# Output projection of the first attention block on 64-row tiles, in two-step turns with sixteen row maxima; 32 turns with six

## The chip, the core and the metric

The kernel runs on one core of a Trainium2 chip. TensorE (PE) multiplies into PSUM, VectorE (DVE) and ScalarE (ACT) read PSUM, GpSimd (POOL) works on SBUF only, SyncE (SP) issues the DMAs. PSUM has eight banks of 128 x 512 float32. The metric is the device time in microseconds (us), as the median of several runs. The profile is one execution of the same program.

## What is computed

Two attention blocks on inputs of 2048 tokens and width 512, with 32 heads of 16 channels. Block A sees a window of 256 tokens, block B sees all 2048. The results stand side by side.

```python
qkv = (x @ wqkv).reshape(B, S, 3, H, Dh).transpose(2, 0, 3, 1, 4)
scores = einsum("bhqd,bhkd->bhqk", q, k) * Dh ** -0.5    # A: where(mask, scores, -1e9)
o = einsum("bhqk,bhkd->bhqd", softmax(scores), v)
out = o.transpose(0, 2, 1, 3).reshape(B, S, D) @ wo
```

Float32 accuracy comes from splitting operands into a high and a low part: each product of the projections is three matmuls (high x high, high x low, low x high).

## The kernel before

The program has two stages. The first, up to about 518 us, does block A and the projections of both blocks, in an order written out by hand (`ORDER_A`). The second stage, of which the change speaks, is one Python loop that writes out block B's attention: 32 units (8 head groups of 4 heads, 4 chunks of 512 queries), each of 16 key steps of 128 keys, so 512 steps. One turn of the loop covers two steps and follows the string `ORDER`, one letter for each piece of work:

- `s`: one score product, 128 keys x 512 queries of one head (`scores`, a matmul with 51 rows on one 64-row tile of PE), then ScalarE's exponential of the 128x512 block into `p` (L635). Eight in a turn.
- `m`: the row maxima of one head over 512 keys: a matmul with 48 rows on one 64-row tile (`max2`, L471) and VectorE's reduction of 128x512 (L475). `M`: the same for two heads, with one reduction of 128x1024. Four `m` and two `M` are eight maxima in a turn. They belong to the next unit: the scores of a unit need its maxima, which go through GpSimd (`max_chunk`, `max_finish`), a transpose on PE (`max_rows`, L595) and a DMA into `oq`.
- a digit: that many 128-query quarters of a step of the weighted sum of the values (`weigh2`, L659), on four 32-column tiles of PE. Eight quarters in a turn.

Two matmuls on the two 64-row tiles run side by side, so two of `s` and `m` take one slot of PE.

Meanwhile block A's result is projected with `wo`: 16 output tiles of 128 x 512 (`project_out`), each 4 x 3 matmuls with 128 rows (`products`, L222), a copy by ScalarE (L779) and a DMA. When two tiles are due, the loop writes both out after the digit `4` of a turn, 24 matmuls in a row with nothing between. This happens in eight turns. No row maxima are issued during these 24 matmuls.

PSUM in this loop: bank 0 is the weighted sum, banks 1 to 3 go to scores in turn, 4 and 5 to `M`, 6 and 7 to `m` and to the output tiles in turn. A matmul waits until its bank has been read. Each engine works in its own order; nothing is reordered at run time, so a waiting matmul holds up all of PE's queue behind it.

After the last maxima the loop follows the string `LAST`, with block B's first output tiles in it.

Of the kernel before, what the change touches and what calls it, by code (L numbers as in the profile page):

```python
# [41 lines left out]
ORDER = "ssm4mssMs2msms2sM"  # L42
LAST = "4ssssfssss4"
AHEADM = 4
# [37 lines left out]
class Model:  # L82
# [64 lines left out]
    def release(self, bank, t):  # L147
        self.banks[bank[0]][bank[1]] = t + self.load


@with_exitstack
def attention_kernel(ctx: ExitStack, tc: tile.TileContext, xT, wqk, wv, wo, out):
# [190 lines left out]
    def half_rows(stage, pairs, banks):  # L343

        turn, q0 = divmod(CHUNK * stage, 12)
        for q in range(q0, q0 + CHUNK):
            k, i = divmod(q, 3)
            u, v = ((0, 0), (0, 1), (1, 0))[i]
            for a in range(2):
                l, r = pairs[a ^ turn][k]  # L350
                rows = slice(64 * a, 64 * a + 64)
                op = nc.tensor.matmul(view(banks[a ^ turn]), l(u)[rows], r(v)[rows], start=turn == q == 0,  # L352
                                      stop=turn == 1 and q == 11)
                if turn and q == a == 0:
                    tc.add_manual_dep(op.ins, min(since)[2].ins.name, LANDED, reason="the row tiles change banks")
        M.pe("h", CHUNK * 233)

# [89 lines left out]
    def maxima(b, g, c):  # L447

        if not b:
            if (b, g, c) not in mt:  # L450
                xt.reverse()
                mt[b, g, c] = xt[0]
            return mt[b, g, c].rearrange("p a s (r q) -> p a r q s", q=4)
        if (b, g, c) not in mt:
            m = sb.tile([128, NQC, HG, 4], F32, name=f"mt_{b}_{g}_{c}",
                        **(dict(tag="mte", bufs=1) if (b, g, c) == (1, 0, 0) else dict(tag="mt", bufs=3)))
            mt[b, g, c] = m.rearrange("p k h q -> p h q k")
        return mt[b, g, c]

    def max2(g, c, qt, kc, heads, ps):  # L460

        m = maxima(1, g, c).rearrange("p (a r) q k -> p a r q k", a=2)
        early = g == 0 and c == 0 and heads[0] < 2
        if not early:
            follow(("k", 1, g))
            follow(("q", 1, g, c))
        for n, j in enumerate(heads):
            r, a = divmod(j, 2)
            rows = slice(ROW[a], ROW[a] + KS)
            q, k = (qe[0], ke()) if early else (opq[1, g, c][:, r], opk2(g)[:, r])  # L470
            nc.tensor.matmul(ps[:, n], q[rows, 128 * qt:128 * qt + 128], k[rows, kc * QC:kc * QC + QC], start=True,  # L471
                             stop=True)
            t = M.pe("h", 118, 0 if early else loaded(1, g, c))
        r, a = divmod(heads[0], 2)
        op = nc.vector.tensor_reduce(out=m[:, a:a + len(heads), r, qt, kc], in_=ps, axis=AX.X, op=ALU.max)  # L475
        return mark(op, M.run("DVE", 65 + 533 * len(heads), t))
# [23 lines left out]
    def max_item(b, g, c, qt, j, kc):  # L500
        n = f"{b}_{g}_{c}_{qt}_{j}_{kc}"
        if b:
            banks, two = take2()
            release2(banks, max2(g, c, qt, kc, (j, j + 1), two))
# [28 lines left out]
    def max_chunk(b, g, c, kc):  # L533

        n = f"{b}_{g}_{c}"
        m = mt[b, g, c]
        if kc == 1:
            parts["mm"] = sb.tile([128, HG, 4], F32, name=f"mm_{n}", tag="mm")
        mm = parts["mm"]
        x = m[:, :, :, kc]  # L540
        up = sb.tile([128, HG, 4], F32, name=f"mu_{n}_{kc}", tag="mu", bufs=1)
        gt = sb.tile([128, HG, 4], F32, name=f"mg_{n}_{kc}", tag="mg", bufs=1)

        if kc == 1:
            nc.gpsimd.tensor_sub(up, x, m[:, :, :, 0])  # L545
        else:
            nc.gpsimd.tensor_add(up, x, mm)
        nc.gpsimd.tensor_scalar(gt, up, 0.0, None, op0=ALU.is_gt)
        nc.gpsimd.tensor_mul(up, up, gt)
        if kc == 1:  # L550
            nc.gpsimd.tensor_add(up, up, m[:, :, :, 0])
# [5 lines left out]
    def max_finish(b, g, c):  # L557
# [7 lines left out]
        if slot[0]:  # L565
            mr = max_chunk(b, g, c, 3)
            r1 = sb.tile([128, HG, 4], F32, name=f"nr_{n}", tag="nr")
            mr, r1 = (y.rearrange("p (a r) q -> p a (r q)", a=2) for y in (mr, r1))
# [4 lines left out]
        else:  # L573
            if b:
                nc.vector.tensor_reduce(out=x[:, :, 0], in_=mt[b, g, c].rearrange("p (a r) q k -> p a (r q) k", a=2),
# [8 lines left out]
    def max_rows(b, g, c):  # L584
        n = f"{b}_{g}_{c}"
        nm = parts["nm"].bitcast(BF16).rearrange("p a s (n u) -> p a (s n) u", u=2)[:, :, :, 1]
        if slot[0]:

            bank = M.take("e")
            ps = view(bank)  # L590
# [27 lines left out]
    def scores(b, g, c, kt, j, heads=1, pieces=((),)):  # L618
# [3 lines left out]
        banks = [M.take("e" if b else "u") for _ in range(heads)]  # L622
        ps = [view(bank) for bank in banks]
# [10 lines left out]
        for x in range(heads):  # L634
            op = nc.scalar.activation(p[:, a0 + x, :w], ps[x][:, :w], AF.Exp, scale=SCALE)  # L635
            done = mark(op, M.run("ACT", 60 + w / 1.2, t))
            M.release(banks[x], done)
# [124 lines left out]
    def project_out(b, c, qts):  # L762
# [14 lines left out]
        for qt in qts:  # L777
            ob = row(f"ob_{b}_{c}_{qt}")
            nc.scalar.activation(ob, ps[qt], AF.Copy)  # L779
            t = M.run("ACT", 480, M.t["PE"] + WAKE)  # L780
            release(banks[qt], t)
            nc.sync.dma_start(out[c * QC + 128 * qt:c * QC + 128 * qt + 128, b * D:(b + 1) * D], ob)
            M.dma(256, t)
# [211 lines left out]
    for u, (b, g, c) in enumerate(units[:NA + 2]):  # L995
        its = max_items(b, g, c)
        its = its[:HG // 2 * AHEADM] if u > NA else [it for it in its if it[1]] if u == NA else its
# [162 lines left out]
    M.banks["e"] = M.banks["u"][:3]  # L1160
    slot[0] = True
    steps = [(g, c, kt) for _, g, c in units[NA:] for kt in range(NT)]
    turn = len(units) - NA - 1
    mx = [(NA + 1 + i // 16, *units[NA + 1 + i // 16][1:], *divmod(i % 16, NQC)) for i in range(16 * turn)]
    ns, nq, nm, half, got = 0, -8, AHEADM, 0, 0
    t0 = M.t["PE"]
    half_tile = 0
    rows = []
    while nq < 4 * len(steps):
        if nm == len(mx) and len(M.banks["e"]) == 3:  # L1170

            M.banks["e"] += [M.t["PE"] + 3000] * 2
        for x in ORDER if nm < len(mx) else LAST:
            k = ns // HG
            if x == "s" and k < len(steps):
                if ns % HG == 0:
                    t = k * STEP
                    M.t["PE"] = max(M.t["PE"], t0 + int(1000 * k * STEP))
# [3 lines left out]
                scores(1, *steps[k], ns % HG)  # L1182
                ns += 1
            elif x in "Mm" and nm < len(mx):
                if nm == AHEADM and got == 0:
                    for _ in range(FILL):
                        nc.tensor.matmul(ps_all[:, 0, 0:256], mone[:, 0], mone, start=True, stop=True)
                u, g, c, qt, kc = mx[nm]
                if x == "M":
                    h = (0, 1)  # L1190
                    two = view(("p", 0))
                else:
                    h = (2 + half,)
                    half ^= 1
                    two = room()[1][:, None]
                max2(g, c, qt, kc, h, two)
                got += len(h)
                if got == HG:
                    nm += 1
                    got = 0  # L1200
                    if nm % 16 in (14, 15):
                        max_chunk(1, g, c, nm % 16 - 13)
                    if nm % 16 == 0:
                        max_finish(1, g, c)
                        rows.append((k + 1, (1, g, c)))
            elif x == "f" and k < len(steps) and not rows:

                for _ in range(6):
                    if gen[0] or proj and proj[0][0] <= k * STEP and operands(proj[0][3]) <= M.t["PE"]:
                        advance()  # L1210
                        half_tile += 1
# [3 lines left out]
            elif x.isdigit():  # L1215
                if 0 <= nq < 4 * len(steps):
                    g, c, kt = steps[nq // 4]
                    q = nq % 4
                    weigh2(g, c, kt, 128 * q, 128 * (q + int(x)))
                    if kt == NT - 1 and q + int(x) == 4:  # L1220
# [46 lines left out]
```

## Time and profile before

| | |
|---|---|
| device time, median of 3 runs | 1799.53 us (1796.18 to 1802.74) |
| span of the profiled execution | 1797.4 us |
| what lies around the span, by the median | 2.1 us |
| PE, DVE, ACT, POOL busy in the span | 99%, 84%, 78%, 36% |
| second stage, from the first to the last turn with maxima | 520.5 to 1716.3 us |
| an ordinary turn (800 to 986.3 us are 40 of them) | 4.66 us |
| the 40 turns that hold the eight with output tiles | 581.2 to 813.2 us |

The busy share of PE is an upper bound, since the ends of matmuls are modelled. The distance between the starts of two rows is read instead. In a view by order of time a row merges equal instructions that follow each other; it gives the start of the first, the time from there to the end of the last, and their count.

### The profile page before, as it was taken

The page shows a single profiled execution, that of the slowest core. Times are in us where ns is not written, and L with a number is a line of the kernel's source. Part 1 is how long each engine was busy: PE and PEld are TensorE (multiplying, and loading weights), DVE is VectorE, ACT ScalarE, POOL GpSimd, SP SyncE. Part 2 cuts the span into 40 slices and gives each one's busy share as a digit, 9 for nine tenths or more (in the row PEclk, how much of TensorE's full clock was granted, in tenths as well). Part 3 has the DMA queues.
Part 4 walks back from the last instruction along what each step waited for, and adds up shares of the span by engine and source line. Part 5 has one row for each costly group of instructions (what it writes and reads, how often), then busy time and mean ns, then how long its engine had stood idle before and what let it go on. Part 6 is the DMA issues. An engine that isn't in the chain of part 4 may idle for free.

```text
span 1797.4 us, 39182 instructions
## 1 busy us (share of the span) xinstructions
PE 1779.1 (99%) x15054; PEld 907.9 (51%) x15054; DVE 1510.2 (84%) x2244; ACT 1401.6 (78%) x2749; POOL 651.4 (36%) x1334
## 2 busy tenths in 40 slices
PE   8999999999999999999999999999999999999999
PEld 6776657767754555444444444444444444444336
DVE  4766786676789677899999999999999999999911
ACT  4366676665569677899999999999999999999983
POOL 0377888656755331133400024220112422022220
PEclk9999999999999999999999999999999999999999
DMA  7766667645562223211200310130031121010012
GB/s 256 204 204 202 202 203 224 177 143 172 187 183 87 78 86 100 52 41 37 65 17 31 72 34 29 38 70 16 17 77 35 29 64 37 17 54 9 32 37 94
DMA packets 129354, 166.80 MB, mean 93 GB/s; under 512 B 23204, under 2 KB 59044, under 8 KB 129156
## 3 DMA queue, kind: packets, MB, share of 16 engines
q1 hardware_dynamic: 129168, 164.31, 31.0%
q8 instruction: 118, 1.93, 0.4%
q14 instruction: 68, 0.56, 0.1%
HBM read 94.49 MB, written 68.19 MB: 91 GB/s over the span
## 4 chain that ended last, share of the span: by engine, by line
PE 94%; DMA 2%; ACT 1%; DVE 1%; SPq 1%; issue 1%; POOL 0%; ACTq 0%; DVEq 0%
PE ps_all L659 30%; PE ps_all L471 20%; PE ps_all L628 19%; PE ps_all L222 11%; PE ps_all L352 7%; PE ps_all L674 4%; PE ps_all L518 3%; ACT p L635 1%; DMA in<-xT_A 1%; SPq L382 0%; PE ps_all L595 0%; DVE nm L528 0%; DMA in<-xT_B 0%; DVE ps_all L527 0%; DMA vd<-vst 0%
## 5 line engine op out<-in xcount | busy, mean ns | idle before, releaser
L635 ACT ACTIVATE p<-ps_all 128x512 f32<-128x512 f32 x2432 | 1260.9, 597 | 178.8 <-PE ps_all L628 114.6
L475 DVE TENSOR_REDUCE mt<-ps_all 128x2 f32<-128x1024 f32 x1516 | 1195.6, 870 | 63.0 <-PE ps_all L471 63.0
L628 PE MATMUL ps_all<-oq,opk 51*128 51x512 f32 (+2 forms) x2752 | 768.4, 404 | 4.5 <-ACT p L635 2.4
L471 PE MATMUL ps_all<-opk,oq 48*128 48x512 f32 x2016 | 673.3, 438 | 0.2
L659 PE MATMUL ps_all<-p,vt 128*17 128x256 f32 (+1 forms) x6056 | 586.2, 460 | 1.7 <-ACT ou L685 1.7
L628 PEld LDWEIGHTS ps_all<-oq,opk 51*128 51x128 f32 x2752 | 394.6, 185 | 179.0 <-ACT p L635 150.3
L471 PEld LDWEIGHTS ps_all<-opk,oq 48*128 48x128 f32 x2016 | 307.7, 184 | 315.3 <-DVE mt L475 179.5
L645 POOL TENSOR_SCALAR_AFFINE_SELECT p<-p 128x256 f32<-128x256 f32 x480 | 179.8, 409 | 110.7 <-ACT p L635 108.8
L659 PEld LDWEIGHTS ps_all<-p,vt 128*17 128x17 f32 x6056 | 101.5, 95 | 228.1 <-issue 215.7
L545 POOL TENSOR_TENSOR mu<-mt 128x16 f32<-128x16 f32 x31 | 6.9, 221 | 509.3 <-DVE mt L475 509.3
L527 DVE COPY_PREDICATED ps_all<-mone,ps_all 128x256 f32<-128x256 uint16 x224 | 95.3, 426 | 82.0 <-PE ps_all L518 75.4
L528 DVE TENSOR_REDUCE nm<-ps_all 128x2 f32<-128x512 f32 x224 | 155.2, 693 | 7.7
L713 POOL TENSOR_TENSOR rd<-ld,minus 128x32 f32<-128x32 f32 x15 | 81.9, 5460 | 216.4 <-DMA ld<-od 216.4
L352 PE MATMUL ps_all<-x,w 64*128 64x512 f32 x720 | 119.1, 392 | 0.0
L222 PE MATMUL ps_all<-x,w 128*128 128x512 f32 x408 | 104.3, 405 | 2.9 <-ACT x L170 2.2
L674 PE MATMUL ps_all<-p,vt 128*17 128x384 f32 (+2 forms) x1408 | 94.1, 387 | 0.1
L518 PE MATMUL ps_all<-opk,oq 48*128 48x384 f32 (+2 forms) x512 | 91.8, 362 | 2.2 <-DMA oq<-parts 0.7
L222 PE MATMUL ps_all<-w_o,x_o 128*128 128x512 f32 x384 | 92.5, 395 | 0.0
L352 PEld LDWEIGHTS ps_all<-x,w 64*128 64x128 f32 x720 | 84.1, 185 | 8.8
L222 PEld LDWEIGHTS ps_all<-x,w 128*128 128x128 f32 x408 | 75.3, 191 | 25.8 <-ACT x L170 2.9
L305 ACT ACTIVATE raw<-ps_all 128x512 f32<-128x512 f32 x56 | 32.3, 597 | 70.4 <-PE ps_all L222 55.5
L222 PEld LDWEIGHTS ps_all<-w_o,x_o 128*128 128x128 f32 x384 | 70.7, 188 | 25.0 <-issue 8.4
(77 smaller groups left out, 942.2 us busy)
## 6 DMA issues: line engine op xcount, KB each, us to landing
parts<-st SPq DMA_DIRECT2D x64, 512.0 KB
oq<-parts SPq DMA_DIRECT2D x128, 128.0 KB
opk<-parts SPq DMA_DIRECT2D x128, 128.0 KB
od<-ou SPq DMA_DIRECT2D x64, 256.0 KB
vd<-vst SPq DMA_DIRECT2D x32, 272.0 KB
oq<-parts SPq DMA_DIRECT2D x128, 64.0 KB
opk<-parts SPq DMA_DIRECT2D x128, 64.0 KB
t<-od SPq DMA_DIRECT2D x32, 256.0 KB
```

What stands on the lines that cost most here:

```text
L222: nc.tensor.matmul(ps, l(u), r(v), start=start and k == 0, stop=stop and k == n - 1)
L352: op = nc.tensor.matmul(view(banks[a ^ turn]), l(u)[rows], r(v)[rows], start=turn == q == 0, stop=turn == 1 and q == 11)
L471: nc.tensor.matmul(ps[:, n], q[rows, 128 * qt:128 * qt + 128], k[rows, kc * QC:kc * QC + QC], start=True, stop=True)
L475: op = nc.vector.tensor_reduce(out=m[:, a:a + len(heads), r, qt, kc], in_=ps, axis=AX.X, op=ALU.max)
L518: nc.tensor.matmul(two[:, a, 0:w], opq[b, g, c][rows, r, 128 * qt:128 * qt + 128], opk2(g)[rows, r, t0:t1], start=True, stop=True)
L527: nc.vector.copy_predicated(two[:, :, 256:384], later, two[:, :, 0:128])
L528: op = nc.vector.tensor_reduce(out=m[:, :, r, qt, 0], in_=two[:, :, 128:384], axis=AX.X, op=ALU.max)
L628: nc.tensor.matmul(ps[x][:, col:col + n1], opk2(g)[rows, pr, 128 * k:128 * k + 128], opq[b, g, c][rows, pr, q0:q0 + n1], start=True, stop= ...
L635: op = nc.scalar.activation(p[:, a0 + x, :w], ps[x][:, :w], AF.Exp, scale=SCALE)
L645: nc.gpsimd.affine_select(out=v, in_=v, pattern=[[0, 2], [sign, 128]], compare_op=ALU.is_ge, fill=zero_fill, base=base, channel_multiplier ...
L659: nc.tensor.matmul(o[32 * j:32 * j + VW, q0:q1], vt[(g // 2) % 2][:, kt, vc:vc + VW], pts[1, g, c, kt, j // 2][:, j % 2, q0:q1], start=kt ...
L674: nc.tensor.matmul(o[32 * j:32 * j + VW, q0:q0 + w], vt[(g // 2) % 2][:, kt, vc:vc + VW], pts[b, g, c, m, j // 2][:, j % 2, col:col + w], ...
```

## The change

The output tiles of block A are written in pairs on 64-row tiles: a 128-row matmul becomes two with 64 rows, one on each tile of PE (`half_step`, which the first stage had inside `half_rows`). In the first 12 of 24 steps the upper row tile works on the first output tile and the lower one on the second, then they change over; the first matmul after that waits for an operation (the earliest by the planner's clock) issued since, so that both tiles never write one bank. The 24 steps (`g`) stand between the letters of a turn of its own, `OUTS`, with 16 maxima, all of single heads, 8 scores and 8 quarters (two digits `4` in a row). Both tiles are copied by ScalarE behind the last `g` (`put_out`).

Maxima that are thus done early let 32 other turns be `FEW`, with 6 maxima and two digits `4`, while `MANY` is the old `ORDER` unchanged. A turn is `FEW` when the maxima lead the scores by more than 1.25 units (`LEADM`). The program as built has, in order, 14 turns `MANY`, then 40 turns that are 8 `OUTS` and 32 `FEW` (OOFFFFOFOFFFFOOFFFFOFOF and 17 more F), then 192 `MANY` and 10 `LAST`; before, all 246 turns up to `LAST` were `ORDER`.

The maxima of a unit now run with the key chunk as the outer loop, so that `max_chunk` runs after each quarter of a unit and no longer at its end. Banks are chosen by a small model of the engines (`Loop`): scores use banks 1 to 4 in `FEW`, maxima 5 to 7; in `OUTS` both share 1 to 5 and the output tiles hold 6 and 7. `PACES` is a planner's clock that says when loads and other side work are written out.

```diff
-ORDER = "ssm4mssMs2msms2sM"
+MANY = "ssm4mssMs2msms2sM"
+FEW = "msmms4msssmsm4ss"
+OUTS = "mgggmmggmsgggmsgmmgmggmm44smgsmmgggsgsmggmssggmggg"
 LAST = "4ssssfssss4"
-AHEADM = 4
+PACES = {FEW: 2.25, MANY: 2.45, OUTS: 5.4, LAST: 2.45}
+ROOMS = {FEW: (range(4), range(4, 7)), MANY: (range(3), range(5, 7)), OUTS: (range(5), range(5)),
+         LAST: (range(5), range(5))}
+LEADM = 1.25
...
+class Loop:
...
+    def pick(self, rooms, ready=0):
+        n = min(rooms, key=lambda n: (self.free[n], n))
+        return n, max(ready, self.free[n] + self.SEM)
...
+    def half_step(q, pairs, ps):
+
+        turn, q = divmod(q, 12)
+        k, i = divmod(q, 3)
+        u, v = ((0, 0), (0, 1), (1, 0))[i]
+        for a in range(2):
+            l, r = pairs[a ^ turn][k]
+            rows = slice(64 * a, 64 * a + 64)
+            op = nc.tensor.matmul(ps[a ^ turn], l(u)[rows], r(v)[rows], start=turn == q == 0,
+                                  stop=turn == 1 and q == 11)
+            if turn and q == a == 0:
+                tc.add_manual_dep(op.ins, min(since)[2].ins.name, LANDED, reason="the row tiles change banks")
...
+    def put_out(b, c, qt, ps):
+        ob = row(f"ob_{b}_{c}_{qt}")
+        nc.scalar.activation(ob, ps, AF.Copy)
+        t = M.run("ACT", 480, M.t["PE"] + WAKE)
+        nc.sync.dma_start(out[c * QC + 128 * qt:c * QC + 128 * qt + 128, b * D:(b + 1) * D], ob)
...
     while nq < 4 * len(steps):
...
+        two = heapq.nsmallest(2, proj)
+        lead = np_ / 32 - ns / 64
+        if np_ == total:
+            cycle = LAST
+        elif two and two[-1][0] <= ns / HG * STEP and max(operands(x[3]) for x in two) <= M.t["PE"]:
+            cycle = OUTS
...
+        else:
+            cycle = FEW if lead >= LEADM + 1 / 32 else MANY
+        loop.rooms = ROOMS[cycle]
+        for x in cycle:
...
+            elif x == "g":
+                if nh == 12:
+                    ready_h = max(ready_h, loop.first + loop.SEM)
+                half_step(nh, [pairs_out(*y) for y in two], [ps_all[:, 6], ps_all[:, 7]])
...
+                if nh == 12:
+                    since.clear()
+                    loop.first = M.NEVER
+                if nh == 24:
+                    for n1, y in enumerate(two):
+                        put_out(*y, ps_all[:, 6 + n1])
...
-                if int(x) == 4 and nm < len(mx):
-
-                    t = k * STEP
-                    two = heapq.nsmallest(2, proj)
-                    if two and two[-1][0] <= t and max(operands(y[3]) for y in two) <= M.t["PE"]:
-                        now[0] = t
-                        for _ in two:
-                            advance()
-                            while gen[0]:
-                                advance()
-                            t0 += 2400
```

In the rows of the program's order below, `w_o` is a part of `wo`, `x_o` a normalised part of block A's result, `oq` and `opk` the operands of scores and maxima, `p` the exponentials and `vt` the values. What stands in brackets are the engines and DMA queues whose semaphores the row waits for.

On PE, at the first pair of output tiles, before:

```order
L659 MATMUL ps_all<-p_0_1_10_0_7788,vt_77 17x512 x2
L659 MATMUL ps_all<-p_0_1_10_1_7801,vt_77 17x512 x2
L222 MATMUL ps_all<-w_o_6439,x_o_0_0_7299 128x512 [waits DVE_49]
L222 MATMUL ps_all<-w_o_6439,x_o_0_0_7299 128x512 x2
L222 MATMUL ps_all<-w_o_6468,x_o_1_0_7403 128x512 [waits Pool_49]
L222 MATMUL ps_all<-w_o_6468,x_o_1_0_7403 128x512
L222 MATMUL ps_all<-w_o_6468,x_o_1_0_7403 128x512 [waits Pool_49]
```

On PE, at the same pair, now:

```order
L557 MATMUL ps_all<-opk_75,oq_0_3_6956 128x512 [waits DMAHW4_49,DMAHW3_49,Activation_49]
L440 MATMUL ps_all<-w_o_6439,x_o_0_0_7313 128x512 [waits DVE_49] x2
L440 MATMUL ps_all<-w_o_6439,x_o_0_0_7313 128x512 x4
L557 MATMUL ps_all<-opk_75,oq_0_3_6956 128x512 [waits DMAHW6_49,DMAHW5_49,Activation_49]
L557 MATMUL ps_all<-opk_75,oq_0_3_6956 128x512 [waits Activation_49]
L440 MATMUL ps_all<-w_o_6468,x_o_1_0_7346 128x512 x4
L557 MATMUL ps_all<-opk_75,oq_0_3_6956 128x512 [waits DVE_49]
L713 MATMUL ps_all<-oq_0_1_6572,opk_75 128x512
```

The output matmuls (L222, now L440 and twice as many) no longer stand in one run: maxima (L557) and scores (L713) stand between them.

On PE, where the second output tile of a pair begins, before:

```order
L222 MATMUL ps_all<-w_o_6777,x_o_3_0_7568 128x512 [waits Pool_49]
L222 MATMUL ps_all<-w_o_6439,x_o_0_0_7299 128x512 [waits DVE_49]
L222 MATMUL ps_all<-w_o_6439,x_o_0_0_7299 128x512 x2
L222 MATMUL ps_all<-w_o_6468,x_o_1_0_7403 128x512 x3
L222 MATMUL ps_all<-w_o_6686,x_o_2_0_7433 128x512 x3
```

On PE, where the row tiles change over in the same pair, now:

```order
L745 MATMUL ps_all<-p_0_1_11_0_7815,vt_77 17x512 x2
L745 MATMUL ps_all<-p_0_1_11_1_7828,vt_77 17x512 x2
L713 MATMUL ps_all<-oq_0_1_6572,opk_75 128x512 [waits DVE_49]
L557 MATMUL ps_all<-opk_75,oq_0_3_6956 128x512 [waits DVE_49]
L440 MATMUL ps_all<-w_o_6439,x_o_0_0_7313 128x512 [waits Activation_49]
L440 MATMUL ps_all<-w_o_6439,x_o_0_0_7313 128x512
L713 MATMUL ps_all<-oq_0_1_6572,opk_75 128x512 [waits DVE_49]
```

The 13th step waits for ScalarE, with a score two places ahead of it. In four of the eight pairs the 13th step names ScalarE, in the other four VectorE.

On PE, behind the last matmul of a pair of output tiles, before:

```order
L222 MATMUL ps_all<-w_o_6777,x_o_3_0_7568 128x512 x3
L471 MATMUL ps_all<-opk_75,oq_0_3_6956 128x512 [waits DMAHW6_49,DMAHW5_49,Activation_49]
L628 MATMUL ps_all<-oq_0_1_6572,opk_75 128x512 x2
L471 MATMUL ps_all<-opk_75,oq_0_3_6956 128x512 x2
L628 MATMUL ps_all<-oq_0_1_6572,opk_75 128x512
L659 MATMUL ps_all<-p_0_1_11_0_7815,vt_77 17x256 x2
```

On PE, behind the second pair, where a turn `FEW` follows, now:

```order
L440 MATMUL ps_all<-w_o_6777,x_o_3_0_7568 128x512 x6
L557 MATMUL ps_all<-opk_75,oq_0_3_6956 128x512 [waits DVE_49]
L713 MATMUL ps_all<-oq_0_2_6760,opk_75 128x512 [waits DMAHW3_49]
L557 MATMUL ps_all<-opk_75,oq_0_3_6956 128x512 [waits Activation_49] x2
L713 MATMUL ps_all<-oq_0_2_6760,opk_75 128x512 [waits DMAHW4_49]
L745 MATMUL ps_all<-p_0_1_14_0_7997,vt_77 17x512 x2
```

Two maxima that wait for ScalarE now stand among the first four matmuls behind the pair.

## Rows read from the trace of the kernel before

**Rows 1.** First part of the page: busy time, share of the span, instructions.

```profile
PE 1779.1 (99%) x15054; PEld 907.9 (51%) x15054; DVE 1510.2 (84%) x2244; ACT 1401.6 (78%) x2749; POOL 651.4 (36%) x1334
```

**Rows 2.** Two stretches of 40 turns: us, busy PE PEld DVE ACT POOL, clock, DMA.

```profile
581.23:813.18 231.95, 231.95 (x1808) 111.13 (x1804) 187.76 (x241) 177.00 (x347) 66.56 (x126) 1.00 0.25 71
800.00:986.30 186.30, 186.30 (x1614) 75.62 (x1610) 186.30 (x242) 168.86 (x331) 45.13 (x106) 1.00 0.15 39
```

**Rows 3.** DVE by order of time, an ordinary turn: start, us, operation, count.

```profile
1004.31 0.68 DVE L475 TENSOR_REDUCE mt<-ps_all 128x1 f32<-128x512 f32 x1
1004.91 0.68 DVE L475 TENSOR_REDUCE mt<-ps_all 128x1 f32<-128x512 f32 x1
1005.51 1.22 DVE L475 TENSOR_REDUCE mt<-ps_all 128x2 f32<-128x1024 f32 x1
1006.64 0.68 DVE L475 TENSOR_REDUCE mt<-ps_all 128x1 f32<-128x512 f32 x1
```

**Rows 4.** PE by order of time, an ordinary turn.

```profile
1009.03 0.50 PE L471 MATMUL ps_all<-opk,oq 48*128 48x512 f32 x1
...
1009.37 0.39 PE L471 MATMUL ps_all<-opk,oq 48*128 48x512 f32 x1
...
1009.61 0.40 PE L471 MATMUL ps_all<-opk,oq 48*128 48x512 f32 x1
1009.93 0.62 PE L659 MATMUL ps_all<-p,vt 128*17 128x256 f32 x8
1010.49 0.50 PE L471 MATMUL ps_all<-opk,oq 48*128 48x512 f32 x1
...
1011.16 0.63 PE L659 MATMUL ps_all<-p,vt 128*17 128x256 f32 x8
1011.72 0.50 PE L628 MATMUL ps_all<-oq,opk 51*128 51x512 f32 x1
...
1012.64 1.05 PE L659 MATMUL ps_all<-p,vt 128*17 128x512 f32 x8
1013.62 0.49 PE L471 MATMUL ps_all<-opk,oq 48*128 48x512 f32 x1
```

**Rows 5.** A turn with a pair of output tiles, PE, ACT and DVE.

```profile
585.93 5.74 PE L222 MATMUL ps_all<-w_o,x_o 128*128 128x512 f32 x24
...
589.03 0.60 ACT L779 ACTIVATE ob<-ps_all 128x512 f32<-128x512 f32 x1 [2.95 <-POOL nm L569]
...
591.60 0.50 PE L471 MATMUL ps_all<-opk,oq 48*128 48x512 f32 x1
...
592.04 0.60 ACT L779 ACTIVATE ob<-ps_all 128x512 f32<-128x512 f32 x1 [2.41 <-PE ps_all L222]
592.13 3.02 DVE L475 TENSOR_REDUCE mt<-ps_all 128x1 f32<-128x512 f32 x4 [5.41 <-PE ps_all L471]
```

**Rows 6.** DVE's waits from 575 to 770 us: total, times, longest.

```profile
DVE mt L475 <- PE ps_all L471: 44.2, 9, 5.7
```

**Rows 7.** ACT by order of time, exponentials without a pause between.

```profile
1009.60 2.56 ACT L635 ACTIVATE p<-ps_all 128x512 f32<-128x512 f32 x5 [0.41 <-PE ps_all L471]
```

**Rows 8.** First stage, PE by order of time: products on 64-row tiles.

```profile
118.91 1.54 PE L352 MATMUL ps_all<-x,w 64*128 64x512 f32 x12
120.29 0.34 PE L518 MATMUL ps_all<-opk,oq 48*128 48x384 f32 x2
```

**Rows 9.** PE by order of time, a turn with the transpose of a unit's maxima.

```profile
1006.33 0.63 PE L659 MATMUL ps_all<-p,vt 128*17 128x256 f32 x8
1006.92 0.23 PE L595 MATMUL ps_all<-ident,nm 128*32 128x128 bf16 x2
1007.08 0.50 PE L628 MATMUL ps_all<-oq,opk 51*128 51x512 f32 x1
```

More of the change, by code (lines that the diff above doesn't have):

```diff
@@ L343, in half_rows @@
     def half_rows(stage, pairs, banks):
[L345 to L355, printed above, removed]
-        M.pe("h", CHUNK * 233)
+        for q in range(CHUNK * stage, CHUNK * stage + CHUNK):
+            half_step(q, pairs, [view(bank) for bank in banks])
+        M.pe("h", CHUNK * 233)
+    def half_step(q, pairs, ps):
+        turn, q = divmod(q, 12)
+        k, i = divmod(q, 3)
+        u, v = ((0, 0), (0, 1), (1, 0))[i]
+        for a in range(2):
+            l, r = pairs[a ^ turn][k]
[4 more added lines that the diff above has]
+                tc.add_manual_dep(op.ins, min(since)[2].ins.name, LANDED, reason="the row tiles change banks")
     def heads_of(b, g, s, a):
@@ L503, in max_item @@
             banks, two = take2()
-            release2(banks, max2(g, c, qt, kc, (j, j + 1), two))
+            release2(banks, max2(g, c, kc, qt, j // 2, (0, 1), two))
             return
@@ L565, in max_finish @@
         if slot[0]:
[L566 to L568 removed]
+            mr = max_chunk(g, c, 3)
+            r1 = sb.tile([128, 16], F32, name=f"nr_{n}", tag="nr")
+            mr, r1 = (y.rearrange("p (a n) -> p a n", a=2) for y in (mr, r1))
             nc.gpsimd.tensor_copy(nm[:, :, :, 1], mr)
@@ L587, in max_rows @@
         if slot[0]:
-            bank = M.take("e")
-            ps = view(bank)
+            bank, ps = None, ps_all[:, 1 + loop.rows()]
         else:
@@ L621, in scores @@
         pr, a0 = divmod(j, 2)
-        banks = [M.take("e" if b else "u") for _ in range(heads)]
-        ps = [view(bank) for bank in banks]
+        if b:
+            ps = [ps_all[:, 1 + loop.score(a0)]]
+        else:
+            banks = [M.take("u") for _ in range(heads)]
+            ps = [view(bank) for bank in banks]
         w = QC if b else sum(x[3] for x in pieces)
@@ L777, in project_out, with pairs_out @@
         for qt in qts:
[L778 to L783, printed above, removed]
+            release(banks[qt], put_out(b, c, qt, ps[qt]))
+    def put_out(b, c, qt, ps):
[3 more added lines that the diff above has]
+        nc.sync.dma_start(out[c * QC + 128 * qt:c * QC + 128 * qt + 128, b * D:(b + 1) * D], ob)
+        M.dma(256, t)
+        return t
+    def pairs_out(b, c, qt):
+        return [(lambda u, p=p: osp[b, p, c][:, u, 128 * qt:128 * qt + 128], lambda v, p=p: ws[b, "o", p][:, v])
+                for p in range(NG // 2)]
     units = [(b, g, c) for b in range(2) for g in range(NG) for c in range(NQC)]
@@ L1159, in attention_kernel @@
     M.load = 0
-    M.banks["e"] = M.banks["u"][:3]
+    loop = Loop()
     slot[0] = True
     steps = [(g, c, kt) for _, g, c in units[NA:] for kt in range(NT)]
-    turn = len(units) - NA - 1
-    mx = [(NA + 1 + i // 16, *units[NA + 1 + i // 16][1:], *divmod(i % 16, NQC)) for i in range(16 * turn)]
-    ns, nq, nm, half, got = 0, -8, AHEADM, 0, 0
+    total = 32 * NA
+    ns, nq, np_, nf = 0, -8, 40, 0
+    side, other = 1, None
     t0 = M.t["PE"]
```

163 lines of the change are left out of this document (116 added, 47 removed).

## The prediction

> **What bounds the kernel now.** I read the page first, and saw that its shares do not decide: PE is busy for 99% of the span and DVE for 84% [rows 1], and the first is an upper bound. So I read the second stage by stretches of 40 turns. In an ordinary stretch, 186.3 us, DVE is busy for all of it; in the stretch that holds the eight pairs of output tiles it is busy for 187.8 of 231.95 us [rows 2]. Three facts follow.
>
> First, an ordinary turn is DVE's. The starts show .60 us for a single reduction (1004.31 to 1004.91) and 1.13 for a double (1005.51 to 1006.64) [rows 3]. Four and two of them are 4 x .60 + 2 x 1.13 = 4.66, and 186.3 / 40 is 4.66 [rows 2].
>
> Second, PE is hardly behind. In order of time its turn is a run of row-tile matmuls of three slots (1009.03 to 1009.93, .90), a weighted sum of two quarters (.56), two slots (.67), .56, three slots (.92) and a sum of four quarters (.98, 1012.64 to 1013.62), together 4.59 [rows 4]. A slot, two matmuls side by side, is .235 us (1009.37 to 1009.61 is .24); a run of n slots takes about .20 more than n x .235, for the changes of mode at its ends [rows 4].
>
> Third, the pairs leave DVE idle. 24 output matmuls run from 585.93 to 591.60 and DVE's next reduction has waited 5.41 us [rows 5]; all such waits are 44.2 us [rows 6], which is 231.95 - 187.76. That is the most that the change could win.
>
> **The change part by part.** I sum over the same 40 turns, 231.95 us before; they hold 320 maxima before and after (8 x 16 + 32 x 6), and DVE needs 320 x .60 = 192 us for them as singles. Outside, the other 206 turns with maxima and `LAST` keep their contents. The order on every engine up to the first pair is the old one but for the maxima's layout; I cost that at nothing, because the reductions of the same shapes hide it.
>
> *A turn FEW.* DVE falls to 6 x .60 = 3.6 us. ACT needs 8 x .49 = 3.9, since five exponentials take 2.56 us of which the last is .60 [rows 7]. PE has two runs of seven matmuls, which need four slots each (.235 x 4 + .20 = 1.14), and two sums of four quarters (.98): 2 x 2.12 = 4.25. So PE sets it, and a turn gains .41. 32 x 4.25 = 136.0. No row shows such a turn; the bounds are 4.23, with no jitter, and 4.45, if scores also wait for ACT now and then (below).
>
> *A turn OUTS, PE alone.* 24 steps are 24 slots; the twelve half-rows that the first stage runs take 1.38 us to the next row (118.91 to 120.29), .23 a slot [rows 8], so 64-row halves cost the .236 of a 128-row matmul (5.67 / 24, [rows 5]) and nothing is won on PE as such. 16 maxima and 8 scores are 12 slots, and about half a slot goes unused where two neighbours want the same row tile: 36.5 x .235 + .20 = 8.78. Eight quarters in a row are .98 + .88 = 1.86 (the .10 of the way out falls once). 10.64 a turn, 8 x 10.64 = 85.1. DVE's 16 x .60 = 9.6 lies beside it.
>
> *The output banks behind a pair.* This is the term that I look at hardest. Before, the first tile's copy starts at 589.03, under the second tile's matmuls; what follows on PE goes to other banks first, so the second copy, at 592.04, holds up nothing for a while [rows 5]. Now both tiles end with the same slot. A matmul's start to its copy's start is .5 us (half the run is over at 588.77, so the 12th of 24 starts at 588.53, its copy at 589.03), the copy is .60 [rows 5], the next start behind a wait takes .10 longer [rows 4], and the second copy comes .49 later [rows 7]. PE can write the first bank 1.2 and the second 1.7 us after the last step. But the order puts maxima for these banks, or the next pair, one to two slots behind it: some .5. So PE stands still for about 1.2, with everything queued behind. 8 x 1.2 = 9.6; the bounds are .5 a turn, if only one bank is wanted early, and 1.3: 4 to 10.4.
>
> *The changeover.* The 13th step waits for an earlier operation. In four pairs it names ScalarE, with a score two places ahead: .5 to the exponential, .60 for it, .10 more, less the slot that is due anyway: 1.0. In the others it names a reduction that should be old. Where ACT's operation is older than that score, less is left, so I take .6 x 4 = 2.5, between 0 and 8.
>
> *The rest.* The first pair finds both banks in VectorE's hands, and maxima at the ends of `OUTS` turns wait for reductions: 1.5 in all, between 0 and 4. Each unit's transpose lengthens PE's turn from .56 to .75 (1006.33 to 1007.08) [rows 9]; DVE covered that and PE's turns do not: 5 units x .19 = 1.0. The loads that `PACES` moves on SP are the same in number; I cost them at nothing, since units of maxima lead by over one, and a late load would cost one stall of 1 to 2 us.
>
> Sum: 136.0 + 85.1 + 9.6 + 2.5 + 1.5 + 1.0 = 235.7 against 231.95: **+3.8 us**. The span becomes 1801.2, and with the 2.1 us by which the median stands above the profiled span, 1803.3. The change thus trades DVE's idle 44.2 us for PE's limit: PE's pure work would gain 10 us, and new waits eat it.
>
> Two rules of the Trainium skill speak against the change. The pair's copies are seen at 589.03 and 592.04, three microseconds apart [rows 5]. The page TensorEngine Tiling (Array Packing), in Performance Considerations under PSUM Bottleneck, says that tiling speeds up TensorE but not the emptying of PSUM, which may become the limit. By it the term of 9.6 stands; without it the sum would be 226.1, a gain of 5.9. No row of before shows a changeover's wait in this loop. The same page, in Restrictions and Gotchas, Gotcha 1, says that different row tiles cannot use one PSUM bank at the same time and that software has to see to it. By it the changeover's wait cannot be left out; if all eight pairs pay it in full the sum is 241.2.
>
> **The rivals.** *A, the waits are covered.* If copies and the changeover fall under work that PE has anyway, 136.0 + 85.1 + 1.0 = 222.1 is left, -9.9: 1789.7. For it: ACT is idle for half of an `OUTS` turn, so copies start at once. Against it: the order itself, since nothing on PE stands between. 12%.
>
> *B, slower, by the score banks in FEW.* PE issues seven matmuls in a row of which four are scores, on four banks; ACT hands a bank back each .49 us [rows 7], and stands only .35 a turn below PE's 4.25. If ACT starts each half turn late, behind .98 of weighted sums, PE waits some .1 each half turn: 4.45, 32 x .2 = 6.4 more, 1809.7. It decides from .04 a turn upwards, with the sum near the bound. Against it: four banks, and three carry an ordinary turn without a wait in its slots [rows 4]. 22%.
>
> *C, slower, by the changeover*: all eight pairs wait 1.0, +5.5: 1808.8. Against it are the four that name VectorE. 12%.
>
> That the change does not do what it says is ruled out by the order: eight pairs, 384 half-row matmuls.
>
> **How the numbers follow.** Forecast 54%, 1803.3, with its own range 1798 to 1808. A measurement can tell .3%, 5.4 us, from no change: 1794.1 to 1804.9. Of the forecast's 54%, some 41 fall within this and 12 above; A gives 11 below; B and C are mostly above, 9 of their 34 within. So faster 12%, same 50%, slower 38%. The range: with 4, 0 and 0 for the waits the sum ends at 226.1, 1793.7; with B's price on top and the waits at 10.4 and 4, about 1812. I take 1793 to 1812.
>
> **What would show it.** In the changed kernel's trace: `FEW` turns of 4.2 to 4.3 us, with PE and no longer DVE without idle time; `OUTS` turns of 11 to 12.6; behind each pair a stop of PE that ends with ACT's copy, about 1.2; at the 13th step, in four pairs, one that ends with an exponential; ordinary turns still 4.66. The forecast is wrong if `FEW` turns are above 4.4 (B), or if `OUTS` turns come to 10.7 with no stop behind (A). The weakest terms are the stop behind a pair and the price of a `FEW` turn: .1 us in each of the latter is 3.2 us.

## The result and the profile after

The changed kernel takes 1804.26 us (median, 1800.56 to 1809.47) against 1799.49 for the kernel before on the same chip (1796.18 to 1803.50): a ratio of 1.0027, 95% interval 1.0018 to 1.0035. That is 4.8 us slower, just inside the .3% that was called no change, and 1.0 us above the forecast. The profiled execution has a span of 1802.6 us (before 1797.4).

First part of the page of the changed kernel:

```profile
PE 1779.8 (99%) x14926; PEld 913.2 (51%) x14926; DVE 1524.2 (85%) x2324; ACT 1403.5 (78%) x2749; POOL 648.6 (36%) x1334
```

Against [rows 1] next to nothing moved: DVE has 80 reductions more and 14 us more of work, PE's busy time is the same within 1 us. The stretch tells more. Two stretches of the changed kernel, from the first maximum of the first turn `OUTS` to the first score of the first `MANY` behind (the same 40 turns as before, with the same 320 maxima), and 186 us behind it (columns as in [rows 2]):

```profile
584.75:820.14 235.39, 230.65 (x1677) 115.25 (x1673) 203.56 (x323) 179.17 (x347) 63.24 (x124) 1.00 0.22 64
820.14:1006.40 186.26, 186.14 (x1607) 75.58 (x1607) 184.17 (x238) 168.59 (x330) 40.86 (x102) 1.00 0.15 38
```

The 40 turns take 235.39 us against 231.95 [rows 2]: +3.44; the sum said 235.7. The rest of the 5.2 us between the spans lies outside: the first pair's turn begins .8 us later, and 1.0 is lost behind 820.14, part of it where the first `MANY` waits for its three score banks. The .8 can't be put down to the change: in the profiles of the experiments below that leave everything ahead of the first pair as it is in the changed kernel, the first output matmul starts between 581.2 and 588.8 us. DVE's idle time in the stretch fell from 44.2 [rows 6] to 235.39 - 203.56 = 31.8 us, and PE, busy without a break before, now has 4.7 us without a matmul even by its modelled ends.

Where that is, is read from starts. PE by order of time behind the second pair, and ACT at the same place:

```profile
608.67 0.86 PE L440 MATMUL ps_all<-w_o,x_o 64*128 64x512 f32 x6
609.65 0.49 PE L557 MATMUL ps_all<-opk,oq 48*128 48x512 f32 x1
609.65 0.49 PE L713 MATMUL ps_all<-oq,opk 51*128 51x512 f32 x1
610.28 0.98 PE L557 MATMUL ps_all<-opk,oq 48*128 48x512 f32 x2
611.10 0.40 PE L713 MATMUL ps_all<-oq,opk 51*128 51x512 f32 x1
611.43 1.05 PE L745 MATMUL ps_all<-p,vt 128*17 128x512 f32 x8
```

```profile
609.63 1.08 ACT L868 ACTIVATE ob<-ps_all 128x512 f32<-128x512 f32 x2 [0.34 <-issue]
```

The last of the three steps in the first row starts at 609.14, .23 apart as always. The next three slots of PE start at 609.65, 610.28 and 610.77 (two maxima merged in one row), 1.63 us for what takes 3 x .235 = .70: a stop of .92. The second and third wait for the two copies, which end at about 610.2 and 610.7 (the first waits for a reduction of VectorE, but that wait ends before the copies do). The views of waits name them by the weight loads: PEld L557 and L440 behind ACT's `ob`, 14 times in the stretch.

PE at the 13th step of the first pair, the changed kernel:

```profile
591.99 0.49 PE L713 MATMUL ps_all<-oq,opk 51*128 51x512 f32 x1
591.99 0.49 PE L557 MATMUL ps_all<-opk,oq 48*128 48x512 f32 x1
593.23 0.50 PE L440 MATMUL ps_all<-w_o,x_o 64*128 64x512 f32 x2 [0.74 <-ACT p L720]
```

The step starts 1.24 us behind the score whose exponential it waits for; without a wait it is .33, as the first slot behind a sum. And a turn `FEW`, PE by order of time:

```profile
749.86 1.05 PE L745 MATMUL ps_all<-p,vt 128*17 128x512 f32 x8
750.84 0.50 PE L713 MATMUL ps_all<-oq,opk 51*128 51x512 f32 x2
...
751.98 1.05 PE L745 MATMUL ps_all<-p,vt 128*17 128x512 f32 x8
752.96 0.50 PE L557 MATMUL ps_all<-opk,oq 48*128 48x512 f32 x1
...
754.10 1.05 PE L745 MATMUL ps_all<-p,vt 128*17 128x512 f32 x8
```

Sum to sum is 2.12 twice, 4.24 a turn, against 4.66 of an ordinary one [rows 2]. The eight `OUTS` turns take 10.4 to 12.6.

### The profile page after: what moved, and what is told of

The parts are those of the page before. It is cut to its first block, busy times and chain, and to the rows that moved or that the text cites. A ratio compares the mean times of both kernels' runs of the same rounds, so it can differ in the third digit from the quotient of the medians.

```text
span 1802.6 us, 39006 instructions
## 1 busy us (share of the span) xinstructions
PE 1779.8 (99%) x14926; PEld 913.2 (51%) x14926; DVE 1524.2 (85%) x2324; ACT 1403.5 (78%) x2749; POOL 648.6 (36%) x1334
## 4 chain that ended last, share of the span: by engine, by line
PE 90%; DVE 5%; ACT 2%; DMA 2%; SPq 1%; issue 1%; POOL 0%; ACTq 0%; DVEq 0%; POOLq 0%
PE ps_all L745 28%; PE ps_all L557 19%; PE ps_all L713 18%; PE ps_all L440 10%; PE ps_all L305 8%; PE ps_all L760 4%; DVE mt L560 4%; PE ps_all L603 3%; ACT p L720 1%; DMA in<-xT_A 1%; DVE nm L613 1%; SPq L469 0%; PE ps_all L677 0%; DVE ps_all L612 0%; ACT ob L868 0%
## 5 line engine op out<-in xcount | busy, mean ns | idle before, releaser
L560 DVE TENSOR_REDUCE mt<-ps_all 128x1 f32<-128x512 f32 (+1 forms) x1596 | 1209.5, 832 | 52.8 <-PE ps_all L557 42.6
L713 PE MATMUL ps_all<-oq,opk 51*128 51x512 f32 (+2 forms) x2752 | 757.6, 406 | 4.0 <-ACT p L720 1.5
L557 PE MATMUL ps_all<-opk,oq 48*128 48x512 f32 x2016 | 672.5, 436 | 2.0 <-ACT ob L868 0.9
L745 PE MATMUL ps_all<-p,vt 128*17 128x256 f32 (+1 forms) x5736 | 576.7, 476 | 1.8 <-ACT ou L771 1.7
L713 PEld LDWEIGHTS ps_all<-oq,opk 51*128 51x128 f32 x2752 | 389.1, 186 | 194.9 <-ACT p L720 156.1
L557 PEld LDWEIGHTS ps_all<-opk,oq 48*128 48x128 f32 x2016 | 311.9, 185 | 305.8 <-DVE mt L560 187.1
L745 PEld LDWEIGHTS ps_all<-p,vt 128*17 128x17 f32 x5736 | 97.2, 95 | 223.5 <-issue 210.8
L631 POOL TENSOR_TENSOR mu<-mt,mm 128x16 f32<-128x16 f32 x62 | 13.7, 220 | 385.4 <-DVE mt L560 385.4
L440 PE MATMUL ps_all<-x,w 64*128 64x512 f32 x720 | 119.2, 393 | 0.0
L440 PEld LDWEIGHTS ps_all<-x,w 64*128 64x128 f32 x720 | 84.5, 185 | 8.8
L440 PE MATMUL ps_all<-w_v,x 64*128 64x512 f32 x432 | 81.1, 391 | 0.0
```

What stands on the lines that cost most here:

```text
L440: op = nc.tensor.matmul(ps[a ^ turn], l(u)[rows], r(v)[rows], start=turn == q == 0, stop=turn == 1 and q == 11)
L557: nc.tensor.matmul(ps[:, a - lo], q[rows, 128 * qt:128 * qt + 128], k[rows, kc * QC:kc * QC + QC], start=True, stop=True)
L560: op = nc.vector.tensor_reduce(out=m[:, kc, lo:lo + len(sides), r, qt], in_=ps, axis=AX.X, op=ALU.max)
L713: nc.tensor.matmul(ps[x][:, col:col + n1], opk2(g)[rows, pr, 128 * k:128 * k + 128], opq[b, g, c][rows, pr, q0:q0 + n1], start=True, stop= ...
L745: nc.tensor.matmul(o[32 * j:32 * j + VW, q0:q1], vt[(g // 2) % 2][:, kt, vc:vc + VW], pts[1, g, c, kt, j // 2][:, j % 2, q0:q1], start=kt ...
```

## The experiments

The theory: PE's own work fell by about 10 us, and PE's waits (the copies behind each pair, the changeover, the rest) took it back. The rival: PE's own work did not fall, and the waits only show where it has slack. Where a length "from the first to the last output matmul" is given, it is between the starts of L440 in the eight pairs: 156.2 us in the changed kernel. Ratios are to the kernel before, each with its 95% interval.

**The changeover alone.** The step waits for the operation issued first.

```diff
-                tc.add_manual_dep(op.ins, min(since)[2].ins.name, LANDED, reason="the row tiles change banks")
+                tc.add_manual_dep(op.ins, min(since, key=lambda x: x[1])[2].ins.name, LANDED, reason="the row tiles change banks")
```

> One part changed: the 13th step of each pair waits for the operation that was issued first since the 12th step, and no longer for the one that the planner's clock puts earliest. Theory (PE's own work is some 10 us less, and PE's waits eat it; the changeover is one of them): in the changed kernel's trace the 13th step follows its predecessor after 1.235 us in two pairs and .43 in two more, against .33 without a wait, so 2 x .90 + 2 x .10 = 2.0 us lie there. With an older operation named all eight gaps are .33 and the time is about 2 us under the changed kernel, 1802. Rival 1 (the two long gaps are covered, because what DVE or ACT does next sets the end): the gaps go and the time stays, 1804. Rival 2 (the wait is passed on: PE meets the next bank the earlier): the gaps go, a like amount turns up behind the pair, 1804.

Measured: 1800.86 us, ratio 1.0006 (.9995 to 1.0016), 3.4 under the changed kernel; first to last output matmul 153.7, 2.5 less. PE at the same place of this kernel:

```profile
592.54 0.49 PE L713 MATMUL ps_all<-oq,opk 51*128 51x512 f32 x1
592.54 0.50 PE L557 MATMUL ps_all<-opk,oq 48*128 48x512 f32 x1
592.87 0.40 PE L440 MATMUL ps_all<-w_o,x_o 64*128 64x512 f32 x2
```

All eight gaps are .33 to .34. The stops behind the pairs kept their size (476 + 652 + 486 ns behind the second pair, 507 + 630 + 488 in the changed kernel): nothing is passed on. The instructions' order is the old one; only in the four pairs that named ScalarE do waits differ.

**The late changeover.** The same line with `max(since)`.

> One part changed the other way: the 13th step waits for the operation that the planner's clock puts last since the 12th step, so that all eight pairs pay the changeover. Theory: each pair pays 1.0 as the two pairs do that wait for a young exponential (a gap of 1.235 against .33), so the six others add .9 each less what they pay now: 5 to 6 us over the changed kernel, 1809 to 1810. That was the prediction's rival C. If the wait in such a place is covered by DVE or ACT, the time stays at 1804 to 1805.

Measured: 1842.35 us, ratio 1.0237 (1.0219 to 1.0255), +38. This expectation missed, because it overlooked that the first stage's 24 pairs of products (1152 matmuls of this line, 48 a pair; the next expectation says 28) use the same line: that stage ends 32 us later. Its view of waits of PE (total us, times, longest) has, among others,

```profile
PE ps_all L440 <- DVE nm L613: 14.5, 12, 1.3
PE ps_all L440 <- ACT p L720: 6.3, 5, 1.3
```

and none of L440 in the changed kernel. The eight pairs themselves went from 156.2 to 162.3. To have them alone, the rule was then made late in the second stage only:

```diff
-    def half_step(q, pairs, ps):
+    def half_step(q, pairs, ps, late=False):
...
-                tc.add_manual_dep(op.ins, min(since)[2].ins.name, LANDED, reason="the row tiles change banks")
+                tc.add_manual_dep(op.ins, (max if late else min)(since)[2].ins.name, LANDED, reason="the row tiles change banks")
...
-                half_step(nh, [pairs_out(*y) for y in two], [ps_all[:, 6], ps_all[:, 7]])
+                half_step(nh, [pairs_out(*y) for y in two], [ps_all[:, 6], ps_all[:, 7]], True)
```

> The late wait of e2_last_since in the second stage alone: only the 13th step of the eight pairs of output tiles waits for the operation that the planner's clock puts last, and the first stage, whose 28 pairs of products use the same line, keeps its rule. Theory: the pairs' part of e2_last_since, which its trace shows as 162.3 us from the first to the last output matmul against 156.2 in the changed kernel: +6.1, 1810. The other 32 us of that kernel's 38 were the first stage's. Rival: the first stage's wait was no part of it, and this kernel too takes 1840.

Measured: 1813.45 us, ratio 1.0075 (1.0049 to 1.0101); first to last output matmul 162.4, +6.3, with eight gaps of 1.30 to 1.37. The theory holds in the trace. The median is 3 above 1810: the mean granted clock of these runs is .992 to .999 (median .995), and the two at .999 took 1806.2 and 1807.9. The profiled one has its longest stretch at the lower clock between 200 and 220 us, in the first stage.

**The copies doubled.** ScalarE copies each tile twice behind a pair (`nc.scalar.activation(ob, ps, AF.Copy)` written out twice there).

> The suspected cost doubled: behind each pair of output tiles ScalarE copies each tile twice into the same buffer, 16 more copies of 128x512 in all, everything else as in the changed kernel. Theory (PE's stop behind a pair is set by these copies): the first bank comes free .49 us later and the second .98 later, and PE, which stands for .87 now, stands for 1.85: 8 x .98 = 7.8 over the changed kernel, and up to 4 more where the next pair's or turn's scores then wait for exponentials that stand behind the copies: 1812 to 1816. Rival (the stop is a change of mode or a wait that only ends at the same time; ScalarE is idle for half the turn): 1804 to 1805.

Measured: 1822.28 us, ratio 1.0132 (1.0106 to 1.0157), +18. The direction is the theory's, the size is not. ACT and PE of this kernel behind the third pair:

```profile
638.51 2.34 ACT L869 ACTIVATE ob<-ps_all 128x512 f32<-128x512 f32 x4 [0.23 <-PE ps_all L440]
```

```profile
639.79 0.49 PE L557 MATMUL ps_all<-opk,oq 48*128 48x512 f32 x1 [0.72 <-ACT ob L869]
640.90 0.50 PE L557 MATMUL ps_all<-opk,oq 48*128 48x512 f32 x1 [0.62 <-ACT ob L869]
```

A second copy to the same buffer comes .63 behind the first and not .49 (two copies take 1.08, four 2.34: 1.26 / 2), so the stop grows by 1.25 in six pairs; in the sixth and seventh it grows by only .30 and .43: 8.3 us in all. The other part goes with TensorE's clock. Four stretches of this kernel (PEclk is the third column from the end):

```profile
650.00:660.00 10.00, 9.19 (x76) 5.86 (x72) 9.29 (x15) 5.64 (x11) 0.39 (x1) 1.00 0.12 37
660.00:670.00 10.00, 9.31 (x41) 3.25 (x41) 5.31 (x9) 6.31 (x13) 3.54 (x8) 0.64 0.43 157
670.00:680.00 10.00, 10.00 (x41) 3.78 (x37) 4.69 (x8) 5.68 (x11) 3.90 (x4) 0.51 0.21 67
680.00:690.00 10.00, 10.00 (x77) 6.08 (x76) 8.75 (x15) 7.52 (x15) 4.05 (x7) 1.00 0.18 66
```

From about 663 to 680, behind the fourth pair and its stop, PE ran at the lower of its two levels, 1.2 GHz; two shorter stretches lie between 630 and 650 (mean granted clock .83) and between 730 and 780 (.97 and .79). In the long one a turn `FEW` took 7.68 us (sums at 668.66, 672.50 and 676.35) instead of 4.24. The changed kernel has no such stretch among its pairs. All runs of this kernel have a mean clock of .987 to .995.

**The second copy on VectorE.**

```diff
-        nc.scalar.activation(ob, ps, AF.Copy)
+        if n:
+            nc.vector.tensor_copy(ob, ps)
+        else:
+            nc.scalar.activation(ob, ps, AF.Copy)
...
-                        put_out(*y, ps_all[:, 6 + n1])
+                        put_out(*y, ps_all[:, 6 + n1], n1)
```

> The suspected cost cut: of the two copies behind each pair the second is VectorE's, so that both tiles leave their banks side by side. Theory: the second bank comes free up to .49 us earlier, 8 x .49 = 3.9 less at most; VectorE, which has 16 reductions in such a turn and .60 us more of work then, starts that copy some .1 to .3 late and hands the next maxima's banks back later by as much: 1.5 to 3.5 under the changed kernel, 1801 to 1803. Rival (VectorE is the engine that everything behind the pair waits for): 16 x .60 = 4.8 us on its path, 1805 to 1809.

Measured: 1801.84 us, ratio 1.0013 (1.0004 to 1.0022), 2.4 less. PE of this kernel behind the second pair:

```profile
606.47 0.49 PE L557 MATMUL ps_all<-opk,oq 48*128 48x512 f32 x1
607.12 0.56 PE L557 MATMUL ps_all<-opk,oq 48*128 48x512 f32 x2 [0.16 <-ACT ob L871]
```

The three starts are 513, 649 and 68 ns apart: the first copy still stops PE, the second no longer. So it is in six pairs, each .24 to .40 shorter. Behind the sixth and seventh PE now waits for a reduction that stands behind VectorE's copy, and they are .36 and .41 longer; the sixth:

```profile
693.14 0.50 PE L557 MATMUL ps_all<-opk,oq 48*128 48x512 f32 x1 [0.49 <-ACT ob L871]
693.81 0.50 PE L557 MATMUL ps_all<-opk,oq 48*128 48x512 f32 x1 [0.17 <-DVE mt L560]
```

The time is as the theory said. But the trace shows only 1.2 us less behind the eight pairs together; where the rest of the 2.4 lies is not shown, and it is within the two intervals.

**The sums split.** One of the two sums behind the last output matmul; the letters are the only edit.

```diff
-OUTS = "mgggmmggmsgggmsgmmgmggmm44smgsmmgggsgsmggmssggmggg"
+OUTS = "mgggmmggmsgggmsgmmgmggmm4smgsmmgggsgsmggmssggmggg4"
```

> One part moved: in a turn with output matmuls the second digit 4 stands behind the last g and no longer beside the first, so that .98 us of weighted sums, which use another bank, lie on PE between the last output matmul and the next maxima. Nothing is added or left out. Theory: behind each pair PE stands for about .87 us (gaps of 507 + 630 + 488 ns for three starts that take 3 x 235 without a wait), and .98 of work cover it: up to 8 x .87 = 7 less, if nothing new waits; .1 to .2 of it may go to one more change of mode each turn (8 x .20 = 1.6), and the 13th step now meets operations half a sum younger. 1798 to 1802. Rival (the stop is not one of the copies, or it is passed on to the 13th step): 1804 or more, with gaps at the 13th step of over 1 us in more pairs than two.

Measured: 1802.09 us, ratio 1.0014 (1.0004 to 1.0024), 2.2 less. Both sides were half right. Behind the pairs the stop is gone, but the wait moved: the 13th step of this kernel's first pair,

```profile
591.50 0.49 PE L713 MATMUL ps_all<-oq,opk 51*128 51x512 f32 x1
592.74 0.50 PE L440 MATMUL ps_all<-w_o,x_o 64*128 64x512 f32 x2 [0.74 <-ACT p L720]
```

has a gap of 1.24, and so have all eight, where the changed kernel had it in two. The score now stands directly behind the one sum that is left there, and the planner names its young exponential each time.

**Both waits covered.** Sums ahead of the 13th step and behind the last, and a score earlier; the rule is that of the first experiment.

```diff
-OUTS = "mgggmmggmsgggmsgmmgmggmm44smgsmmgggsgsmggmssggmggg"
+OUTS = "mgggmmggmsgggmsgmmgmggsm4mmgsmgggsgsmggmsggmgggsm4"
```

> Both waits at once: the order of the letters in a turn with output matmuls is mgggmmggmsgggmsgmmgmggsm4mmgsmgggsgsmggmsggmgggsm4 (the same 16 maxima, 24 steps, 8 scores and two sums; a sum ahead of the 13th step and one behind the last, with a score and a maximum between), and the 13th step waits for the operation issued first since the 12th. Theory: the 2 us of the changeover and some 7 us behind the pairs go, less .20 a turn for one more change of mode (1.6): 1795 to 1799, below the kernel before (1799.5). Rival (PE's own work is more than was reckoned, and the waits beside it are small): 1802 to 1804, with PE's gaps gone and the turns no shorter.

Measured: 1792.90 us, ratio .9964 (.9953 to .9974): 11.4 under the changed kernel and 6.8 under the kernel before beside it (1799.71), below the range of the expectation. The letters alone do it: with them the old rule names the same operations, and the program is the same with either. The 40 turns and the place behind the second pair in this kernel, PE and ACT:

```profile
582.50:808.64 226.14, 225.49 (x1678) 112.52 (x1674) 201.29 (x323) 179.39 (x346) 63.30 (x123) 1.00 0.23 67
```

```profile
603.14 0.87 PE L440 MATMUL ps_all<-w_o,x_o 64*128 64x512 f32 x6
603.83 0.39 PE L557 MATMUL ps_all<-opk,oq 48*128 48x512 f32 x1
603.85 0.39 PE L713 MATMUL ps_all<-oq,opk 51*128 51x512 f32 x1
604.17 1.05 PE L745 MATMUL ps_all<-p,vt 128*17 128x512 f32 x8
605.15 0.49 PE L557 MATMUL ps_all<-opk,oq 48*128 48x512 f32 x1
```

```profile
604.10 1.08 ACT L868 ACTIVATE ob<-ps_all 128x512 f32<-128x512 f32 x2 [0.57 <-PE ps_all L440]
```

The same copies, 1.08 us, now lie under a sum of .98 that needs bank 0. 226.14 is 9.25 less than the changed kernel's stretch and 5.8 less than before's. These 9.25 are what the letters are shown to give: between the two profiles another 2.3 us lie ahead of the stretch, where the program is the same, and 1.2 behind it.

**Without the other half.** From that kernel, pairs with 8 maxima, so that no turn is `FEW`.

> From the kernel in which both waits are covered (e4_both_covered), without the other half of the change: a turn with output matmuls has 8 maxima instead of 16, so no turn has six, and all turns outside the pairs hold eight as before. (The letters are mgggmgggmgggmgggsm4sgggsgsggmssggsmggggms4.) Theory (the idle time that VectorE has in the pairs is worth what FEW turns save): eight pairs lose 8 maxima each, 4 slots of .235 us, 7.5 us less on PE; 32 turns go back from 4.25 to 4.66, 13.1 us more: +5.6 against e4_both_covered, 1798 to 1799, about the kernel before. Rival (PE is the bound everywhere, so that moving maxima from one turn to another changes nothing): 1793.

Measured: 1800.83 us, ratio 1.0009 (.9997 to 1.0021), 7.9 above the kernel with both waits covered. The theory holds, with 2 us more than it said. Of these, 1.3 are the pairs', which became .78 shorter and not .94 (8.59 us against 9.37 from a pair's first to its last output matmul, on average); the rest is within the intervals. Row-tiled pairs with all waits covered are worth nothing by themselves; what they are worth is the 32 shorter turns.

**Seventeen maxima.** From the same kernel, one more.

> From e4_both_covered, with one maximum more in each turn with output matmuls, 17 for 16 (mgggmmggmsgggmsgmmgmggsm4mmgsmmgggsgsmggmsggmgggsm4), which lets four more turns have six. Theory: 8 x .12 us for half a slot more on PE, 4 x .41 us less in the turns: -.7 against e4_both_covered, 1792.2; an effect that the measurement can hardly tell. Rival (VectorE, with 17 x .60 = 10.2 us of reductions in a turn of some 10.9, makes PE wait for banks): 1794 to 1796.

Measured: 1795.14 us, ratio .9982 (.9973 to .9992), 2.2 more than with 16. The rival's number, but not shown to be its reason: in the trace the pairs take 149.1 against 147.0 from the first to the last output matmul, .26 a pair, about a whole slot for the odd maximum where half was reckoned, and what follows them is only .6 shorter.

**Three score banks in `FEW`.** `FEW: (range(3), range(4, 7))` in `ROOMS`.

> The prediction's rival B made true: in a turn with six maxima the scores have three banks instead of four, in the changed kernel. Theory (PE sets such a turn only because four banks are enough): four scores lie in a run of seven matmuls, and the fourth now waits until the first one's exponential is done, .50 to its start, .60 for it and .10 to the next matmul, 1.2 us behind the first, where three slots put it .7 behind: up to .5 us a run, two runs a turn, 32 turns: 20 to 32 us over the changed kernel, turns of 4.9 to 5.25, 1824 to 1836. Rival (ScalarE's pace of 3.9 us a turn sets it, and waits in one run are made up in the next): turns below 4.45, 1804 to 1810.

Measured: 1828.57 us, ratio 1.0160 (1.0130 to 1.0190), +24. PE of this kernel in a turn `FEW`:

```profile
761.32 1.05 PE L745 MATMUL ps_all<-p,vt 128*17 128x512 f32 x8
762.30 0.49 PE L557 MATMUL ps_all<-opk,oq 48*128 48x512 f32 x1
762.30 0.73 PE L713 MATMUL ps_all<-oq,opk 51*128 51x512 f32 x3
...
763.52 0.50 PE L713 MATMUL ps_all<-oq,opk 51*128 51x512 f32 x1 [0.25 <-ACT p L720]
...
763.95 1.05 PE L745 MATMUL ps_all<-p,vt 128*17 128x512 f32 x8
...
766.54 1.05 PE L745 MATMUL ps_all<-p,vt 128*17 128x512 f32 x8
```

The fourth score starts 1.22 behind the first of its run, and a turn takes 766.54 - 761.32 = 5.22. Rival B's mechanism is real; the fourth bank is what kept it away.

## Why the prediction came out right, term by term

In short: the mechanism was right, and the sum came within .4 us of the stretch in part by luck, because two sizes that were off cancelled.

**`FEW` turns (136.0): right.** 4.24 where 4.25 stood, and PE sets them. The .41 gained a turn was taken from PE's rows alone, and the missing bank shows how narrow that was: PE's 4.24 holds while four banks stand behind the scores.

**`OUTS` turns, PE alone (85.1): right.** Pairs without a wait take 10.20 from the first to the last output matmul; with the slots of the maximum ahead and of the last step itself (.47) 10.67 against 10.64. That 64-row halves cost a slot each, so that nothing is won on PE as such, holds too.

**The output banks behind a pair (9.6): mechanism right, size too large.** The three starts behind the eight pairs lose .91, .92, .87, .91, .87, .77, .67 and .87, in order, against .235 a slot: 6.8 us, inside the bounds of 4 and 10.4. The step that was off is "PE stands still for about 1.2". Behind the second pair the start on the first bank comes 1.14 us behind the last step and the start on the second 1.63, close to the 1.2 and 1.7 that were reckoned; but the second bank's start is the third behind the last step and due only .70 behind it, not some .5, which leaves .92. The rule of the Trainium skill that was set against the change (TensorEngine Tiling (Array Packing), Performance Considerations, PSUM Bottleneck) agrees with the trace in that emptying PSUM costs PE these 6.8 us. Its premise, a TensorE made faster by tiles, does not hold for the output matmuls (.23 a slot against .236): the wait is there because both tiles end in one slot. Its advice in the same place, to empty PSUM with ScalarE and VectorE together, agrees in six of the eight pairs, by .24 to .40 each, and not in the other two.

**The changeover (2.5): right.** (.6 x 4 is 2.4; the .1 changes nothing.) Two gaps of 1.24 and two of .43 against .33 are 2.0 us; taking them away gave 2.5 in the trace. Two of the four pairs that name ScalarE wait for an older operation, as was reckoned with .6. Rival C's price of 5.5 for all eight is borne out: 6.3 when they were made to pay.

**The rest and the transposes (2.5): too small.** What is left of 235.39 after 135.8, 85.4, 6.8 and 2.0 is 5.4. Some 2.5 of it lie inside pairs (the first takes 1.1 more than 10.20 with its changeover taken off, the second and the sixth .5 each), the remainder mostly in the `FEW` turns at the ends of units, which take 4.4 to 4.7. This excess of 2.9 and the stop's shortfall of 2.8 cancel: that the sum came out within .4 us is luck as far as these two terms go. The 1.8 of the 5.2 us that lie outside the 40 turns had been put at nothing; of them the 1.0 behind 820.14 has the wait of the first `MANY` in it, and for the rest no cause is shown.

**Rival A (1789.7) was a matter of the letters.** "Nothing on PE stands between" was the argument against it, and putting a sum between gave 1792.9 and a stretch of 226.1, against A's 222.1. Of the 4 us that A lacked, 1.6 are one more change of mode a turn by the estimate of .20 [rows 4]; some 1.0 is the first pair's turn (11.86 where the other seven take 10.74 to 10.91), and 1.5 lies in the `FEW` turns, most of it in three that take 4.69 to 4.83. The theory stands, with a smaller size: without the waits the 40 turns of the changed kernel's order would take some 224.5 (226.1 less the 1.6), so PE's own work fell by some 7 us against 231.95, not by 10, and the waits took more than that. That VectorE's 44 us of idle time are what pays is shown by the pairs with eight maxima.

What stays open: where in the first, second and sixth pairs the 2.1 us go was not tried, nor what makes three `FEW` turns longer, nor the split sums with the rule of the first experiment, nor a 17th maximum with a partner.

## What to carry to other kernels

When work is interleaved to fill an idle engine, price the places where a buffer changes hands as separate terms, and look in the order for what stands directly behind each of them: here the places of a few letters in a string decided between 4.8 us lost and 6.8 won. Covering one such wait can push it onto the next one, so cover both and look at both. A rule that is used in two places must be changed in one of them only, or the experiment measures the other.

## What was not expected of the hardware

Longer stops of PE (1.25 us more behind six pairs) came with stretches at 1.2 GHz between the pairs. From the first output matmul to the end that kernel takes 23.5 us more than the changed one, of which the stops are 8.3; the other 15 fit the stretches at the lower clock, some 34 us between 630 and 780 at about half the pace. With the changed kernel's own stops no stretch at that level shows there; why longer stops bring them is not shown. And most of what the runs of one kernel differ by goes with the mean granted clock: the changed kernel took 1809.47 us at .995 and 1800.81 at 1.000.
